# Another head for an attention + MLP kernel: loads by head, masks in fewer passes, weights behind values, and two engines in written order until the third pair

## The chip, the core and the metric

The kernel runs on one core of a Trainium2 chip. The metric is the device time of one execution in microseconds (us). The core has five engines that run side by side and meet at semaphores: TensorE (PE; its weight loads are shown apart as PEld), VectorE (DVE), ScalarE (ACT), GpSimd (POOL) and SyncE (SP), which here issues nearly all transfers. Lower is better.

## The reference

Attention of 4 batches x 8 heads x 768 positions x 64, with a mask and a bias by distance, followed by a two-layer MLP with a gate:

```python
scores = scale * np.matmul(q, k.transpose(0, 1, 3, 2))
keep = is_global | is_local            # first 8 keys, or the last 96 positions up to the query
scores = scores + bias                 # -slope[h] * distance
scores = np.where(keep, scores, -1000000000.0)
a = np.exp(scores - np.max(scores, axis=-1, keepdims=True))
attn = np.matmul(a / (np.sum(a, axis=-1, keepdims=True) + 1e-09), v)
x = attn.transpose(0, 2, 1, 3).reshape(B * S, H * D)      # 3072 x 512
h = x @ w_in                                              # 512 -> 2048
out = (h * np.clip(h + 3.0, 0.0, 6.0) / 6.0) @ w_out      # 2048 -> 512
```

The numbers `n_global` and `n_local` arrive as data, so the masks are built on the chip from a small transfer (`iv`).

## The kernel before, in words

The 3072 rows are 8 blocks of 384 rows (three tiles of 128). Attention of a block is done by pairs of heads, four pairs to a block, so pairs 0 to 11 are the first three blocks (`EARLY` = 12). For each tile t of a pair there are these steps:

- `scores(t)`: TensorE multiplies queries and keys of both heads (L765); VectorE adds the distances `p0` or `p1` of each head and takes the row's least value in one instruction (L776); ScalarE takes the exponential and the row's sum (L780).
- `sum_up` and `normalize`: VectorE adds 1e-9 and takes the reciprocal (L788, L789); the rows are multiplied by it, on VectorE for pair 0 (L796) and on GpSimd for all others (L798).
- `turn(t)`: TensorE transposes the rows (L806, L808), ScalarE copies them out (L810).
- `values`: TensorE multiplies with the values (L850), ScalarE and VectorE split the result into a high and a low part (L150, L151).

The first pairs run in a skewed loop `for n in range(-2, EARLY + 1)`: turn n holds `distances(n + 2)` (for n + 2 < 4), `scores` of pair n + 2, `sum_up` and `normalize` of pair n + 1, `turn` of pair n and `values` of pair n - 1. `distances` scales the masks `d0` and `d1` by each head's slope: three of pair 0's four on ScalarE (L323), all others on GpSimd (L325).

In the head before that loop, `rooms` zeroes half of the query columns of three load buffers on VectorE (L281), `iv` is fetched on ScalarE's queue, the first loads are issued on SP (three transfers for each pair: keys, queries of head 0, queries of head 1), and `banded_masks` makes `d0` and `d1` on VectorE (L263 to L274).

Meanwhile the MLP's weights are decoded: 32 chunks of 512 KB (`wst`, fetched on SP, two buffers), each by a magnitude on ScalarE (L362), six VectorE passes (L381, L394, L400, L409, L384, L398), a copy on ScalarE (L406) and a last VectorE pass (L391). Chunk 2f belongs to the first layer of slice f (`first`, L164), chunk 2f + 1 to the second (`second`, L196). A ledger (`work`) decides where in the written program a decode step stands: the first one stands at the values of turn n = 2. Chunk i + 2 can be fetched only after L384 of chunk i has read its buffer.

What sets the order: TensorE, SP and GpSimd keep the written order from the loop on (`in_order`). ScalarE and VectorE are ordered by the compiler's scheduler, which plays the program through on a timeline of its own and lets whatever is ready there go first. On the chip each engine then runs its list strictly in that order.

From turn n = 8 on, slices of the first block's MLP stand between the pairs; after the pairs, the MLPs of blocks 0 and 1 run, then blocks 2 to 7 with the next block's attention between their slices.

Of the kernel before, what the change touches and what calls it, by code (L numbers as in the profile page):

```python
# [33 lines left out]
QW = 2 * TB  # L34
VW = 2 * NT * P
LOAD = KW + QW + VW
NEG = 1.0e9
# [7 lines left out]
ROOMS = 2  # L45
MORE = 3
LEAD = 5.0
FIRST = 5

# [7 lines left out]
class Kernel:  # L57
# [189 lines left out]
    def banded_masks(self, pool):  # L247


        nc = self.nc  # L250
        c = self.const
        d0 = self.d0 = c.tile([P, P], F32, name="d0")
        d1 = self.d1 = c.tile([P, W], F32, name="d1")
        glo = c.tile([P, NG], F32, name="glo")
        rel, far = (pool.tile([P, W], F32, name=name) for name in ("rel", "local"))
        iota = dict(allow_small_or_imprecise_dtypes=True)
        nc.gpsimd.iota(far[:, CB:W], pattern=[[-1, P]], base=0, channel_multiplier=1, **iota)
        nc.gpsimd.affine_select(out=rel[:, CB:W], in_=far[:, CB:W], compare_op=ALU.is_ge, fill=FAR, base=0,
                                pattern=[[-1, P]], channel_multiplier=1)
# [3 lines left out]
        nc.vector.tensor_copy(out=fv, in_=self.iv)  # L263
        ng, nl = fv[:, 0:1], fv[:, 2:3]
        ts, tt = nc.vector.tensor_scalar, nc.vector.tensor_tensor
        ts(out=glo, in0=glo, scalar1=ng, scalar2=FAR, op0=ALU.is_ge, op1=ALU.mult)
        for d, cols in ((d0, slice(CB, W)), (d1, slice(0, W))):
            ts(out=far[:, cols], in0=rel[:, cols], scalar1=nl, scalar2=FAR, op0=ALU.is_ge, op1=ALU.mult)
            tt(out=d, in0=rel[:, cols], in1=far[:, cols], op=ALU.max)
            if d is d0:  # L270
                ts(out=glo, in0=glo, scalar1=nl, scalar2=None, op0=ALU.max)
                tt(out=d[:, 0:NG], in0=d[:, 0:NG], in1=glo, op=ALU.min)
            else:
                nc.vector.tensor_copy(out=d[:, PREV:CB], in_=glo)  # L274

    def rooms(self, pool, n, start=0):

        room = [pool.tile([P, LOAD], F32, name=f"load{start + i}") for i in range(n)]
        for i, at in enumerate(room):
            for j in range(2):  # L280
                self.nc.vector.memset(at[(1 - j) * D:(2 - j) * D, KW + j * TB:KW + (j + 1) * TB], 0.0)  # L281
        return room

# [3 lines left out]
    def load(self, n, values):  # L287


        if n < len(self.blocks) * NPAIR:  # L290
            parts = [(slice(KW + QW, LOAD), slice(None))] if values else [(slice(0, KW + QW), slice(None))]
            if n < EARLY and not values:
                parts = [(slice(0, KW), slice(None))] + [(slice(KW + j * TB, KW + (j + 1) * TB), slice(j * D, (j + 1) * D)) for j in range(2)]
            for columns, rows in parts:
                self.nc.sync.dma_start(out=self.place(n)[rows, columns], in_=self.pairs[n, rows, columns])

# [7 lines left out]
    def loaded(self, n):  # L304


        at = self.place(n)
        q = at[:, KW:KW + QW].rearrange("p (j t c) -> p j t c", j=2, t=NT)
        v = at[:, KW + QW:LOAD].rearrange("p (s t c) -> p s t c", s=2, t=NT)
        return at[:, 0:KW], q, v[:, 0], v[:, 1]  # L310

# [27 lines left out]
    def banded_setup(self):  # L339
# [3 lines left out]
        self.blocks = [(b, tb) for b in range(B) for tb in range(NTB)]  # L343
        self.room = self.rooms(self.const, ROOMS)
        self.iv = self.const.tile([P, 4], I32, name="iv")
        nc.scalar.dma_start(out=self.iv, in_=self.bounds.broadcast_to([P, 4]))
# [4 lines left out]
        with self.tc.tile_pool(name="scratch", bufs=1) as pool:  # L351
            self.banded_masks(pool)


# [103 lines left out]
    def banded(self, flag):  # L458

        self.banded_setup()  # L460
# [102 lines left out]
        self.finish()  # L563
        self.in_order(start)
        return acc

    def in_order(self, start):

        last = {}
        for i in self.nc.cur_bb.bb.instructions[start:]:  # L570
            if i.engine in (mybir.EngineType.PE, mybir.EngineType.SP, mybir.EngineType.Pool) and "Tile" not in type(i).__name__:
# [3 lines left out]
                last[i.engine] = i.name  # L575

# [136 lines left out]
class Pair:  # L713
# [14 lines left out]
    def split(self, step, load=True):  # L728
# [5 lines left out]
        for j, part in enumerate(self.parts):  # L734
# [3 lines left out]
            if step == 0:  # L738
                part["q1"] = kk.hp.tile([P, NT, P], F32R, name="q1")
                part["q2"] = kk.hp.tile([P, NT, P], F32R, name="q2")  # L740
                part["kx"] = kk.hp.tile([P, KW], F32R, name="kx")
                nc.scalar.mul(out=part["q1"], in_=q[:, j], mul=scale)
                nc.gpsimd.tensor_scalar(out=part["kx"][own, c], in0=k[own, c], scalar1=1.0, scalar2=0.0,  # L743
                                        op0=ALU.mult, op1=ALU.add)
            elif step == 1:
                nc.vector.scalar_tensor_tensor(out=part["q2"], in0=q[:, j], scalar=scale, in1=part["q1"].bitcast(F32),
                                               op0=ALU.mult, op1=ALU.subtract)
# [6 lines left out]
    def scores(self, t):  # L754
# [8 lines left out]
        for j in range(2):  # L763
            if self.plain:
                nc.tensor.matmul(sp[:, j, lo:W], lhsT=queries[:, j, t], rhs=keys[:, c], start=True, stop=True)  # L765
            else:
# [105 lines left out]
def pair_loads(q, k, v):  # L872

    pairs = np.zeros((B * NTB * NPAIR, P, LOAD), q.dtype)
    tile_rows = lambda p: np.concatenate([np.arange(p - PREV, p), np.arange(NG)]).clip(0)
    n = 0
    for b in range(B):  # L880
        for a in range(0, S, TB):
            cols = np.concatenate([np.arange(a - PREV, a).clip(0)]
                                  + [np.concatenate([np.arange(NG), np.arange(p, p + P)]) for p in range(a, a + TB, P)])
            for h in range(0, H, 2):
                qt, kt = (x[b, h:h + 2].transpose(0, 2, 1) for x in (q, k))
                at = pairs[n]
                at[:, 0:KW] = kt[:, :, cols].reshape(P, KW)
                for j in range(2):
                    for half in range(2):
                        if n >= EARLY or half == j:  # L890
                            at[half * D:(half + 1) * D, KW + j * TB:KW + (j + 1) * TB] = qt[j, :, a:a + TB]
                vt = v[b, h:h + 2].transpose(1, 0, 2).reshape(S, P)
# [35 lines left out]
```

## Time and profile before

| | |
|---|---|
| median of 3 runs | 675.11 us (674.5 to 675.69) |
| the profiled execution | 674.97 us, its span 673.1 us, clock 0.998 |
| TensorE busy | 655.3 us, 97% of the span |
| VectorE busy | 438.3 us, 65% |
| ScalarE busy | 283.0 us, 42% |
| GpSimd busy | 192.9 us, 29% |
| first matmul | 4.22 us after the span's start |

Times of the trace are counted from the span's start. TensorE's busy time is modelled from pipelined matmuls, so a busy TensorE is not always one at its peak; its idle time, 17.8 us, is the more telling number. A row of the timeline gives start, length, engine, line, operation, output and input, and in brackets how long the engine had been idle and who ended the wait; rows are merged where the same operation follows itself.

### The profile page before, as it was taken

How to read it: one execution, taken by the hardware profiler on the slowest of the kernel's cores; microseconds unless marked ns; L12 is line 12 of the kernel's file. 1: busy time of each engine (PE TensorE's matmuls, PEld its weight loads, DVE VectorE, ACT ScalarE, POOL GpSimd, SP SyncE). 2: the span in 40 equal slices, each digit the busy share in tenths (PEclk: the TensorE clock that was granted, in tenths of full speed). 3: DMA queues.
4: the chain of work that ended last, by engine and by line, in shares of the span. 5: the costliest groups of instructions: out<-in, count | busy, mean ns of one | idle time of the engine just before them, and what ended most of it. 6: DMA issues, size and time to landing. Idle time of an engine off the chain costs nothing.

```text
span 673.1 us, 11323 instructions
## 1 busy us (share of the span) xinstructions
PE 655.3 (97%) x3905; PEld 588.5 (87%) x3905; DVE 438.3 (65%) x1186; ACT 283.0 (42%) x744; POOL 192.9 (29%) x354
## 2 busy tenths in 40 slices
PE   5999999999999999999999999999999999999996
PEld 4788889999999889899989999899989999989995
DVE  7789999999975666457653676447762666422221
ACT  6998755544446333144333433143331443131111
POOL 2765500000000443234340343315431343302110
PEclk9999999999999999999999999999999999999999
DMA  8677533333303456624654367534555255510001
GB/s 259 164 226 242 162 121 102 118 108 112 95 31 133 131 135 181 157 94 131 167 139 119 101 172 193 144 94 126 139 159 140 80 151 141 139 48 1 1 1 52
DMA packets 62611, 84.33 MB, mean 125 GB/s; under 512 B 8784, under 2 KB 48720, under 8 KB 62544
## 3 DMA queue, kind: packets, MB, share of 16 engines
q1 hardware_dynamic: 62256, 83.25, 43.1%
q8 instruction: 33, 0.54, 0.3%
q14 instruction: 34, 0.28, 0.1%
q10 hardware_dynamic: 288, 0.26, 0.1%
HBM read 62.52 MB, written 20.97 MB: 124 GB/s over the span
## 4 chain that ended last, share of the span: by engine, by line
PE 87%; DMA 4%; ACT 4%; DVE 2%; POOL 2%; issue 1%; SPq 0%; POOLq 0%; ACTq 0%
PE hp L164 38%; PE acc L196 32%; DMA wst<-w 4%; PE xp L850 2%; PE sp L769 2%; PE tp L850 2%; PE sp L196 2%; PE tp L196 2%; PE xp L196 2%; PE tp L769 2%; ACT n L780 2%; POOL n L798 1%; PE acc L765 1%; ACT pt L810 1%; PE acc L850 1%
## 5 line engine op out<-in xcount | busy, mean ns | idle before, releaser
L175 ACT ACTIVATE g<-hp,small 128x384 f32<-128x384 f32 x127 | 73.9, 582 | 256.2 <-PE hp L164 221.2
L164 PE MATMUL hp<-xh,w1h 128*128 128x384 f32 x512 | 174.0, 340 | 0.0
L164 PE MATMUL hp<-xh,w1l 128*128 128x384 f32 x512 | 172.8, 337 | 0.0
L164 PE MATMUL hp<-xl,w1h 128*128 128x384 f32 x512 | 171.9, 336 | 0.0
L182 POOL TENSOR_SCALAR gh<-g 128x384 fp32r<-128x384 f32 x96 | 57.8, 602 | 294.8 <-DVE g L176 264.9
L196 PE MATMUL acc<-w2h,gl 128*128 128x512 f32 x336 | 132.9, 395 | 0.1
L196 PE MATMUL acc<-w2l,gh 128*128 128x512 f32 x336 | 132.8, 395 | 0.0
L196 PE MATMUL acc<-w2h,gh 128*128 128x512 f32 x336 | 132.1, 393 | 0.0
L798 POOL TENSOR_SCALAR n<-n,sums 128x232 f32<-128x232 f32 (+1 forms) x186 | 105.0, 581 | 52.3 <-DVE sums L789 38.7
L176 DVE SCALAR_TENSOR_TENSOR g<-g,hp 128x384 f32<-128x384 f32 x128 | 70.2, 548 | 76.4 <-ACT g L175 75.9
L780 ACT ACTIVATE n<-n,least 128x232 f32<-128x232 f32 (+1 forms) x192 | 89.5, 468 | 39.2 <-DVE least L776 38.5
L189 DVE TENSOR_TENSOR gl<-g,gh 128x384 fp32r<-128x384 f32 x128 | 73.1, 571 | 45.7 <-POOL gh L182 44.1
L164 PEld LDWEIGHTS hp<-xh,w1h 128*128 128x128 f32 x512 | 96.3, 188 | 5.5 <-issue 1.5
L164 PEld LDWEIGHTS hp<-xl,w1h 128*128 128x128 f32 x512 | 96.2, 188 | 3.8
L164 PEld LDWEIGHTS hp<-xh,w1l 128*128 128x128 f32 x512 | 96.0, 188 | 0.0
L196 PEld LDWEIGHTS acc<-w2l,gh 128*128 128x128 f32 x336 | 63.0, 188 | 13.3
L196 PEld LDWEIGHTS acc<-w2h,gl 128*128 128x128 f32 x336 | 63.2, 188 | 11.8 <-DVE gl L189 1.5
L196 PEld LDWEIGHTS acc<-w2h,gh 128*128 128x128 f32 x336 | 63.3, 188 | 10.6 <-POOL gh L182 0.3
L823 DVE STREAM_TRANSPOSE blocks<-n 128x256 f32<-128x256 f32 x112 | 43.5, 424 | 25.7 <-POOL n L798 25.1
L743 POOL TENSOR_SCALAR kx<-load 64x504 fp32r<-64x504 f32 (+1 forms) x40 | 23.1, 577 | 119.2 <-PE hp L164 117.6
L776 DVE CUSTOM_DVE_ANT_0 n<-sp,d 128x232 f32<-128x232 f32 (+1 forms) x70 | 23.7, 376 | 37.1 <-PE sp L769 36.8
L780 ACT ACTIVATION_READ_ACCUMULATOR n<-n,least 128x1 f32 x192 | 36.5, 190 | 0.0
(111 smaller groups left out, 764.9 us busy)
## 6 DMA issues: line engine op xcount, KB each, us to landing
wst<-w SPq DMA_DIRECT2D x32, 512.0 KB, 3.5
there<-blocks SPq DMA_DIRECT2D x52, 256.0 KB, 2.6
load<-pairs SPq DMA_DIRECT2D x20, 636.0 KB, 5.3
load<-pairs SPq DMA_DIRECT2D x32, 384.0 KB, 4.1
weights<-there SPq DMA_DIRECT2D x48, 192.0 KB, 3.8
out<-o SPq DMA_DIRECT2D x23, 256.0 KB, 2.1
weights<-there SPq DMA_DIRECT2D x32, 160.0 KB, 3.3
load<-pairs SPq DMA_DIRECT2D x12, 252.0 KB, 4.5
```

What stands on the lines that cost most here:

```text
L164: self.nc.tensor.matmul(hp, lhsT=self.w1(w, f)[:, kt, :], rhs=a[:, kt, :], start=(n == 0), stop=(n == 3 * NKT - 1))
L175: nc.scalar.activation(out=g, in_=hp, func=AF.Relu, bias=self.three, scale=1.0)
L176: nc.vector.scalar_tensor_tensor(out=g, in0=g, scalar=6.0, in1=hp, op0=ALU.min, op1=ALU.mult)
L182: self.nc.gpsimd.tensor_scalar(out=gh, in0=g, scalar1=1.0, scalar2=0.0, op0=ALU.mult, op1=ALU.add)
L189: self.nc.vector.tensor_tensor(out=gl, in0=g, in1=gh.bitcast(F32), op=ALU.subtract)
L196: self.nc.tensor.matmul(acc[tt], lhsT=a[:, tk], rhs=self.w2(w, f), start=(f == 0 and j == 0), stop=(f == NF - 1 and j == 2))
L769: nc.tensor.matmul(sp[:, j, lo:W], lhsT=q[:, t], rhs=part["kx"][:, c], start=(m == 0), stop=(m == 1))
L776: nc.vector.tensor_tensor_reduce(out=e[:, j, lo:W], in0=sp[:, j, lo:W], in1=d, op0=ALU.add, op1=ALU.min, scale=scale, scalar=3.0e38, accum ...
L780: nc.scalar.activation(out=e[:, j, lo:W], in_=e[:, j, lo:W], func=AF.Exp, bias=self.least[:, i:i + 1], scale=-1.0, accum_out=self.sums[:, ...
L798: nc.gpsimd.tensor_scalar(out=e[:, j, lo:W], in0=e[:, j, lo:W], scalar1=over, scalar2=0.0, op0=ALU.mult, op1=ALU.add)
L823: nc.vector.transpose(out=blocks[:, :, s].rearrange("p b j q -> p j b q"), in_=e[:, :, c:c + P].rearrange("p j (b q) -> p j b q", b=4))
L850: nc.tensor.matmul(xps[j * D:(j + 1) * D, t * P:(t + 1) * P], lhsT=vt[0:K, t, j * D:(j + 1) * D], rhs=self.part(t, j, c, K), start=(c == 0 ...
```

## The change

- The load buffer is laid out anew: queries of head 1, keys, queries of head 0. So each head's keys and queries are one contiguous run of columns in that head's 64 partitions, and a pair's load is two transfers instead of three, each to 64 partitions. For pair 0 the second goes on ScalarE's queue.
- The zeroing moves: two memsets of buffer 0 stay on VectorE, those of buffers 1 and 2 go to GpSimd.
- The masks: the comparison with `n_local` is one VectorE pass over 232 columns instead of two (128 and 232); the two small passes over `glo` and a copy go to GpSimd.
- `wake` issues four small matmuls on a constant before any data is there.
- SP's order: loads of pair 2, values of pair 0, weights chunk 0, values of pair 1, weights chunk 1 (before: chunk 0, loads of pair 2, chunk 1, values of pairs 0 and 1).
- ScalarE and VectorE keep the written order from the very start until turn n = 1 begins (`HEAD` = 1), which is up to the scores of pair 2, the sums of pair 1 and the transposes of pair 0; everything later on these two engines comes behind that.

```diff
+KQ = TB + KW
+HEAD = 1
+WAKE = 4
@@ banded_masks
-        ts(out=glo, in0=glo, scalar1=ng, scalar2=FAR, op0=ALU.is_ge, op1=ALU.mult)
-        for d, cols in ((d0, slice(CB, W)), (d1, slice(0, W))):
-            ts(out=far[:, cols], in0=rel[:, cols], scalar1=nl, scalar2=FAR, op0=ALU.is_ge, op1=ALU.mult)
-            tt(out=d, in0=rel[:, cols], in1=far[:, cols], op=ALU.max)
-            if d is d0:
-                ts(out=glo, in0=glo, scalar1=nl, scalar2=None, op0=ALU.max)
-                tt(out=d[:, 0:NG], in0=d[:, 0:NG], in1=glo, op=ALU.min)
-            else:
-                nc.vector.tensor_copy(out=d[:, PREV:CB], in_=glo)
+        pool_ts = nc.gpsimd.tensor_scalar
+        pool_ts(out=glo, in0=glo, scalar1=ng, scalar2=FAR, op0=ALU.is_ge, op1=ALU.mult)
+        pool_ts(out=glo, in0=glo, scalar1=nl, scalar2=0.0, op0=ALU.max, op1=ALU.add)
+        ts(out=far, in0=rel, scalar1=nl, scalar2=FAR, op0=ALU.is_ge, op1=ALU.mult)
+        tt(out=d0, in0=rel[:, CB:W], in1=far[:, CB:W], op=ALU.max)
+        tt(out=d0[:, 0:NG], in0=d0[:, 0:NG], in1=glo, op=ALU.min)
+        tt(out=d1[:, 0:PREV], in0=rel[:, 0:PREV], in1=far[:, 0:PREV], op=ALU.max)
+        tt(out=d1[:, CB:W], in0=rel[:, CB:W], in1=far[:, CB:W], op=ALU.max)
+        nc.gpsimd.tensor_copy(out=d1[:, PREV:CB], in_=glo)
@@ rooms
-        for i, at in enumerate(room):
-            for j in range(2):
-                self.nc.vector.memset(at[(1 - j) * D:(2 - j) * D, KW + j * TB:KW + (j + 1) * TB], 0.0)
+    def blank(self, room, engine):
+        engine.memset(room[D:P, KQ:KW + QW], 0.0)
+        engine.memset(room[0:D, 0:TB], 0.0)
@@ load
-                parts = [(slice(0, KW), slice(None))] + [(slice(KW + j * TB, KW + (j + 1) * TB), slice(j * D, (j + 1) * D)) for j in range(2)]
+                parts = [(slice(TB, KW + QW), slice(0, D)), (slice(0, KQ), slice(D, P))]
             for columns, rows in parts:
-                self.nc.sync.dma_start(out=self.place(n)[rows, columns], in_=self.pairs[n, rows, columns])
+                engine = self.nc.scalar if n == 0 and rows == slice(D, P) else self.nc.sync
+                engine.dma_start(out=self.place(n)[rows, columns], in_=self.pairs[n, rows, columns])
@@ banded_setup
         self.room = self.rooms(self.const, ROOMS)
+        self.blank(self.room[0], nc.vector)
...
             self.banded_masks(pool)
+        self.blank(self.room[1], nc.gpsimd)
+    def wake(self):
+        any_ = self.three.broadcast_to([P, P])
+        out = self.ps_x.tile([P, BANK], F32, name="xp")[:, 0:P]
+        for _ in range(WAKE):
+            self.nc.tensor.matmul(out, lhsT=any_, rhs=any_, start=True, stop=True)
@@ banded
+        begin = here()
         self.banded_setup()
-        start = len(self.nc.cur_bb.bb.instructions)
+        start = here()
...
+        self.wake()
...
-            self.fetch(0)
...
+                self.blank(self.room[2], self.nc.gpsimd)
                 self.load(2, False)
+                self.load(0, True)
+                self.fetch(0)
+                self.load(1, True)
                 self.fetch(1)
-                for n in range(ROOMS):
-                    self.load(n, True)
...
                 for n in range(-2, EARLY + 1):
+                    if n == HEAD:
+                        head = here()
...
-        self.in_order(start)
+        self.in_order(start, here(), (mybir.EngineType.PE, mybir.EngineType.SP, mybir.EngineType.Pool))
+        self.in_order(begin, head, (mybir.EngineType.Activation, mybir.EngineType.DVE), True)
```

More of the change, by code (lines that the diff above doesn't have):

```diff
@@ L265, in banded_masks @@
         ts, tt = nc.vector.tensor_scalar, nc.vector.tensor_tensor
[L266 to L282 removed]
+        pool_ts = nc.gpsimd.tensor_scalar
[7 more added lines that the diff above has]
+        nc.gpsimd.tensor_copy(out=d1[:, PREV:CB], in_=glo)
+    def rooms(self, pool, n, start=0):
+        return [pool.tile([P, LOAD], F32, name=f"load{start + i}") for i in range(n)]
+    def blank(self, room, engine):
+        engine.memset(room[D:P, KQ:KW + QW], 0.0)
+        engine.memset(room[0:D, 0:TB], 0.0)
     def place(self, n):
@@ L307, in loaded @@
         at = self.place(n)
-        q = at[:, KW:KW + QW].rearrange("p (j t c) -> p j t c", j=2, t=NT)
+        q = [at[:, c].rearrange("p (t c) -> p t c", t=NT) for c in (slice(KQ, KW + QW), slice(0, TB))]
         v = at[:, KW + QW:LOAD].rearrange("p (s t c) -> p s t c", s=2, t=NT)
-        return at[:, 0:KW], q, v[:, 0], v[:, 1]
+        return at[:, TB:KQ], q, v[:, 0], v[:, 1]
     def plain_distances(self, ctx):
@@ L458, in banded @@
     def banded(self, flag):
+        here = lambda: len(self.nc.cur_bb.bb.instructions)
+        begin = here()
         self.banded_setup()
-        start = len(self.nc.cur_bb.bb.instructions)
+        start = here()
         self.common(2, 2)
@@ L563, in banded, with in_order @@
         self.finish()
-        self.in_order(start)
+        self.in_order(start, here(), (mybir.EngineType.PE, mybir.EngineType.SP, mybir.EngineType.Pool))
+        self.in_order(begin, head, (mybir.EngineType.Activation, mybir.EngineType.DVE), True)
         return acc
-    def in_order(self, start):
+    def in_order(self, start, end, engines, first=False):
         last = {}
-        for i in self.nc.cur_bb.bb.instructions[start:]:
-            if i.engine in (mybir.EngineType.PE, mybir.EngineType.SP, mybir.EngineType.Pool) and "Tile" not in type(i).__name__:
+        for n, i in enumerate(self.nc.cur_bb.bb.instructions[start:None if first else end], start):
+            if i.engine in engines and "Tile" not in type(i).__name__:
                 if i.engine in last:
@@ L574, in in_order @@
                         mybir.DependencyClass.NoSync, mybir.DependencyReason.DATA), reason="in_order")
-                last[i.engine] = i.name
+                if n < end:
+                    last[i.engine] = i.name
     def attention(self, i, x, first):
@@ L741, in split @@
                 part["kx"] = kk.hp.tile([P, KW], F32R, name="kx")
-                nc.scalar.mul(out=part["q1"], in_=q[:, j], mul=scale)
+                nc.scalar.mul(out=part["q1"], in_=q[j], mul=scale)
                 nc.gpsimd.tensor_scalar(out=part["kx"][own, c], in0=k[own, c], scalar1=1.0, scalar2=0.0,
@@ L745, in split @@
             elif step == 1:
-                nc.vector.scalar_tensor_tensor(out=part["q2"], in0=q[:, j], scalar=scale, in1=part["q1"].bitcast(F32),
+                nc.vector.scalar_tensor_tensor(out=part["q2"], in0=q[j], scalar=scale, in1=part["q1"].bitcast(F32),
                                                op0=ALU.mult, op1=ALU.subtract)
@@ L764, in scores @@
             if self.plain:
-                nc.tensor.matmul(sp[:, j, lo:W], lhsT=queries[:, j, t], rhs=keys[:, c], start=True, stop=True)
+                nc.tensor.matmul(sp[:, j, lo:W], lhsT=queries[j][:, t], rhs=keys[:, c], start=True, stop=True)
             else:
@@ L886, in pair_loads @@
                 at = pairs[n]
-                at[:, 0:KW] = kt[:, :, cols].reshape(P, KW)
+                at[:, TB:KQ] = kt[:, :, cols].reshape(P, KW)
                 for j in range(2):
@@ L890, in pair_loads @@
                         if n >= EARLY or half == j:
-                            at[half * D:(half + 1) * D, KW + j * TB:KW + (j + 1) * TB] = qt[j, :, a:a + TB]
+                            at[half * D:(half + 1) * D, slice(KQ, KW + QW) if j == 0 else slice(0, TB)] = qt[j, :, a:a + TB]
                 vt = v[b, h:h + 2].transpose(1, 0, 2).reshape(S, P)
```

## The prediction, made before the changed kernel was run

> **What bounds the kernel now.** I read the page first, then the windows, then the timeline of the first 25 us.
>
> ```profile
> span 673.1 us, 11323 instructions
> PE 655.3 (97%) x3905; PEld 588.5 (87%) x3905; DVE 438.3 (65%) x1186; ACT 283.0 (42%) x744; POOL 192.9 (29%) x354
> ```
>
> TensorE is idle for 673.1 - 655.3 = 17.8 us; that, and matmuls that run slowly, is all there is to win. The windows (busy time of PE, PEld, DVE, ACT, POOL, then clock, transfer share, GB/s) say where it lies:
>
> ```profile
> 0.00:5.00 5.00, 0.78 (x3) 0.60 (x3) 3.28 (x13) 1.49 (x2) 1.41 (x10) 1.00 0.51 152
> 10.00:15.00 5.00, 2.57 (x16) 1.82 (x15) 4.05 (x23) 4.79 (x18) 0.00 (x0) 1.00 1.03 344
> 15.00:20.00 5.00, 3.87 (x23) 2.74 (x22) 5.00 (x22) 4.64 (x19) 2.88 (x4) 1.00 0.85 237
> 30.00:35.00 5.00, 5.00 (x45) 4.44 (x45) 3.05 (x16) 4.20 (x16) 3.65 (x9) 1.00 0.87 261
> 45.00:50.00 5.00, 4.88 (x43) 3.93 (x44) 3.64 (x16) 5.00 (x18) 3.91 (x8) 1.00 0.79 253
> ```
>
> In the three early stretches TensorE idles 4.22 + 2.43 + 1.13 = 7.8 us; later it is full, and ScalarE beside it (4.20, then 5.00 of 5). So the head is bound by what feeds TensorE. The timeline shows which work that is:
>
> ```profile
> 0.73 0.41 ACTq L346 DMA_DIRECT2D iv<-bounds  x1
> 0.73 3.44 SPq L295 DMA_DIRECT2D load<-pairs  x6
> 1.00 2.89 DVE L281 MEMSET load<- 64x384 f32 x6
> 3.89 0.17 DVE L263 CAST fv<-iv 128x4 f32<-128x4 int32 x1
> ...
> 5.16 0.51 ACT L323 ACTIVATE p<-d 128x128 f32<-128x128 f32 x2 [2.49 <-DVE d L272]
> 5.84 0.29 DVE L776 CUSTOM_DVE_ANT_0 n<-sp,p 128x128 f32<-128x128 f32 x1
> 6.53 2.84 POOL L325 TENSOR_SCALAR p<-d 128x232 f32<-128x232 f32 x9 [4.55 <-DVE d L274]
> 6.96 0.38 ACT L323 ACTIVATE p<-d 128x232 f32<-128x232 f32 x1
> 7.41 0.40 DVE L776 CUSTOM_DVE_ANT_0 n<-acc,p 128x232 f32<-128x232 f32 x1
> ...
> 10.21 0.67 ACT L362 ACTIVATE wz<-wst 128x512 f32<-128x512 f32 x1 [1.78 <-DMA wst<-w]
> 10.91 0.43 DVE L381 TENSOR_SCALAR wz<-wz 128x512 f32<-128x512 f32 x1 [1.12 <-ACT wz L362]
> 11.50 0.40 DVE L776 CUSTOM_DVE_ANT_0 n<-acc,p 128x232 f32<-128x232 f32 x1
> 11.82 0.40 DVE L776 CUSTOM_DVE_ANT_0 n<-acc,p 128x232 f32<-128x232 f32 x1
> 12.14 0.42 DVE L394 TENSOR_SCALAR wz<-wz 128x512 int32<-128x512 int32 x1
> 13.67 0.69 DVE L400 SCALAR_TENSOR_TENSOR wz<-wst,wz 128x512 int32<-128x512 int32 x1
> 13.91 0.64 ACT L362 ACTIVATE wz<-wst 128x512 f32<-128x512 f32 x1
> 14.27 0.59 DVE L796 TENSOR_SCALAR n<-n,sums 128x232 f32<-128x232 f32 x2
> 15.61 0.42 DVE L381 TENSOR_SCALAR wz<-wz 128x512 f32<-128x512 f32 x1
> 15.95 0.42 DVE L409 TENSOR_SCALAR we<-wz 128x512 int32<-128x512 int32 x1
> 16.91 0.16 DVE L789 RECIPROCAL sums<-sums 128x2 f32<-128x2 f32 x1
> 17.12 4.30 POOL L798 TENSOR_SCALAR n<-n,sums 128x128 f32<-128x128 f32 x6 [7.75 <-DVE sums L789]
> 21.50 1.94 POOL L325 TENSOR_SCALAR p<-d 128x128 f32<-128x128 f32 x4
> 21.84 0.29 DVE L776 CUSTOM_DVE_ANT_0 n<-sp,p 128x128 f32<-128x128 f32 x1 [1.18 <-POOL p L325]
> 24.41 0.68 PE L806 MATMUL tp<-ident,n 128*128 128x128 f32 x2 [0.15 <-POOL n L798]
> ```
>
> The reader is to see two things. ScalarE stands 1.78 us before weights that nothing needs yet (10.21), with pair 0's remaining exponentials queued behind it, and VectorE stands 1.12 us behind that. And GpSimd idles 7.75 us until VectorE gives pair 1's sums; then its own chain runs without a break: normalizing pair 1 (17.12), the distances of pair 3 (21.50), normalizing pair 2, for which TensorE's transposes wait at 24.41. What brings 17.12 forward brings 24.41 forward.
>
> **The change, part by part, counted to GpSimd's start at 17.12.** The first answer on transfers comes ahead (size, us from issue to landing), with two rows of TensorE:
>
> ```profile
> load<-pairs SPq DMA_DIRECT2D x1, 252.0 KB, 3.0
> iv<-bounds ACTq DMA_DIRECT2D x1, 2.0 KB, 3.1
> ...
> load<-pairs SPq DMA_DIRECT2D x1, 252.0 KB, 7.4
> ```
> ```profile
> 5.48 3.06 PE L765 MATMUL acc<-load 128*128 128x232 f32 x8
> 8.82 1.73 PE L765 MATMUL acc<-load 128*128 128x232 f32 x8
> ```
>
> *Memsets and masks.* `iv`, issued at 0.73, lands at 3.83; the six memsets end at 3.89, so taking four off VectorE wins only 0.06. `d0` needs one pass of 232 columns where it had passes of 128 and 8; I put L323 at 5.1 instead of 5.16. The rest of `d1` has one pass less on VectorE, so the first L776 starts near 5.5 instead of 5.84. More matters that ScalarE's scaling of `d1` for head 0 no longer stands behind exponentials (6.96 to 7.34): in written order it runs from about 5.65, and the second tile's L776 starts near 6.15 instead of 7.41: **1.26 us**. The small passes over `glo` lie on an idle GpSimd (4.55 us before 6.53). So do its four memsets: between 4 x 0.38 = 1.5 us (VectorE's 64x384, 2.89 for six with their gaps) and 4 x 0.52 = 2.1 us (a pass of L325, 2.84 / 9 = 0.32, by 384 / 232 columns). I take nothing, since they depend on nothing and can run in that gap; the other end, 2.1 us, is for the case that they stand behind the masks.
>
> *Written order.* No decode step is written before turn n = 2, so all of it leaves the head. VectorE loses the wait of 1.12 and five passes, which cost 0.4 to 0.6 each: **2.1 us**. And pair 1's first sums come ahead of one tile of pair 2's L776 (0.64, two at the pitch 11.50 to 11.82). Together 1.26 + 1.12 + 2.1 + 0.64 = 5.1 us. The same forward from 6.15: pair 0's two tiles, four L776 at 0.32, 1.28; turn n = -1 with six L776 (1.7), three sums (1.0, an estimate from L789's 0.16 twice) and three normalizations (3 x 0.59); then pair 2's first tile and pair 1's sums, 0.75. That ends at 12.65, 4.5 us before 17.12; the 0.6 between the two is what the mixed order overlapped. I take 4.5. ScalarE keeps up: its exponentials of pairs 0 to 2 and three copies end near 16.3.
>
> *Transfers and TensorE's start.* Pair 0's second part goes out on ScalarE's queue behind `iv` near 1.15 and lands near 4.2; the third transfer of before went out near 1.9 (3.44 / 6 each) and landed near 4.9. That wins little, for early matmuls are slow: eight passes take 3.06 us, later 1.73. Slow, the third tile's scores end near 8.3, where VectorE wants the last of them near 7.3 (6.15, three pitches of 0.32 and a semaphore's delay): 1.0 us lost. If `wake` (eight passes of 128 columns, 3.06 x 128 / 232 = 1.7 us, from 1.0 on) has TensorE fast by 4.5, nothing is lost. I take half, 0.5: GpSimd starts near 13.1, **4.0 us** earlier (ends 3.5 and 5.1; 1.9 with the memsets misplaced).
>
> [...]
>
> *Weights behind values.* Chunk 0 was there at 10.21; pair 2's load (252 KB of keys and 2 x 64 x 384 x 4 bytes, 444 KB) and pair 0's values (128 x 768 x 4 bytes) now go ahead, 2.4 us at the 344 GB/s shown. Its cover is that decoding starts behind VectorE's head, near 15. Cost: none.
>
> *What is late next.* The moved decoding must go where the engines are fuller: two magnitudes on ScalarE (0.67 + 0.64 = 1.31 us), some 5 us of passes on VectorE. VectorE has 1.95 us free in 30 to 35, 1.36 in 45 to 50, and a gap from about 15.1 until pair 3's distances at 17.6. ScalarE has 0.80 in 30 to 35 and about 1.3 in that gap. This nearly covers both; I charge 0.4. Sum: 4.0 - 0.4 = **3.6 us**. The profiled execution took 674.97 us (its span and 1.9 around it), 0.14 below the median of 675.11; 675.11 - 3.6 = **671.5 us**.
>
> The shift outlives the pairs only if weights are decoded in time:
>
> ```profile
> 27.54 0.69 DVE L391 TENSOR_TENSOR w2l<-we,w2h 128x512 fp32r<-128x512 f32 x1
> ...
> 35.03 0.68 ACT L362 ACTIVATE wz<-wst 128x512 f32<-128x512 f32 x1 [0.83 <-DMA wst<-w]
> ...
> 84.27 0.68 DVE L391 TENSOR_TENSOR w1l<-we,w1h 128x512 fp32r<-128x512 f32 x1
> ...
> 87.12 0.42 PE L164 MATMUL hp<-xh,w1h 128*128 128x384 f32 x1
> ```
>
> Chunk 8 is ready at 84.95 and used at 87.12, the narrowest margin, 2.2 us. But the chain of chunks moves with the head too, since fetches stand in SP's order among loads that wait for TensorE, and it has a hole from chunk 1's end at 28.2 to chunk 2's start at 35.0.
>
> **The rivals.** *Loads by halves land late.* If 64 partitions take data at half the rate, a pair's 444 KB take 2.6 us instead of 1.3 at 344 GB/s, and pair 3's load (now issued after 8.3, landing 7.4 later, near 15.7; then about 1 us sooner) comes four times 1.3 us later, near 20, where its rows are wanted near 17.5: 2.5 us lost, 674.0. For it: the transfers are saturated there (share 1.03). Against: the halves follow each other and may overlap. [...]
>
> *ScalarE swallows it.* It is full at 45 to 50; if the moved 1.31 us and one more stall before weights, like the 1.78, land there, 3.1 of the 4.0 go: 674.2, no measurable change.
>
> *The decode chain decides (slower).* If chunk 1 ends at 38.5 instead of 28.2, the hole is used up, chunk 8 comes 3.5 us late, its use slips 1.3 us past 87.12 and every block with it: 676.5, and 1 us more for each further us. It takes 10 us of delay, while what moved is some 5 us of passes; unlikely.
>
> **How the numbers follow.** This kernel's runs can tell 0.2%, 1.35 us, from no change. Forecast (2.6 to 5.4 us won) 0.54; half-rate loads or ScalarE taking part of it (1.35 to 2.6 won) 0.20; the same two taking nearly all 0.15; the decode chain 0.11. So faster 0.74, same 0.15, slower 0.11. The low end, 669.7, is the full 5.1 and a little of TensorE's later idling; the high end, 674.8, takes in both swallowing rivals and the misplaced memsets.
>
> **What would show it.** Right: no L362 before 15; GpSimd's first L798 near 13; transposes of pair 2 near 20.4; the L164 of 87.12 some 3.6 us sooner, and likewise all that follows. `wake` right: L765's eight at about 1.8 us instead of 3.06. Wrong: TensorE waiting on `load`, GpSimd's memsets between masks and L325, or L164 waiting for L391 near 83.

## The result, and the profile after

The changed kernel takes **684.88 us** (683.59 to 685.03), where the kernel before, run beside it, took 675.4: a ratio of 1.0133, interval 1.0116 to 1.015. It is 9.5 us slower; 3.6 us faster was forecast. A fourth execution, at a mean granted clock of 0.657, took 922.34 us; it counts in this median (684.74 without it), not in the range or the ratio. The profiled execution took 683.59 us. Page of the changed kernel:

```profile
span 681.6 us, 11332 instructions
PE 659.4 (97%) x3913; PEld 592.7 (87%) x3913; DVE 435.1 (64%) x1179; ACT 283.1 (42%) x744; POOL 192.3 (28%) x361
```

The first three windows of 5 us as before, and 25 to 30 (busy time of PE, PEld, DVE, ACT, POOL, then clock, transfer share, GB/s):

```profile
0.00:5.00 5.00, 2.07 (x8) 1.78 (x8) 1.73 (x7) 1.49 (x2) 3.95 (x17) 1.00 0.55 125
10.00:15.00 5.00, 5.00 (x29) 4.79 (x28) 4.47 (x27) 3.72 (x17) 0.00 (x0) 1.00 1.04 352
15.00:20.00 5.00, 4.55 (x38) 3.44 (x38) 3.44 (x24) 4.62 (x19) 2.99 (x8) 1.00 0.98 250
25.00:30.00 5.00, 2.52 (x18) 1.91 (x14) 5.00 (x18) 4.70 (x19) 0.54 (x1) 1.00 0.73 193
```

From 10 to 20 TensorE is far fuller than before (9.55 against 6.44 us). Then it pays back: 2.52 in 25 to 30, where VectorE has no free time. These rows lie there:

```profile
28.48 0.68 DVE L398 SCALAR_TENSOR_TENSOR we<-wst,we 128x512 f32<-128x512 uint32 x1
29.09 0.18 DVE L812 RECIPROCAL sums<-sums 128x6 f32<-128x6 f32 x1
...
30.13 0.68 PE L829 MATMUL tp<-ident,n 128*128 128x128 f32 x2 [2.60 <-POOL n L821]
```

The transposes of pair 3 wait for GpSimd, GpSimd for pair 3's sums (L812), and VectorE comes to these only behind passes of chunks 0 and 1, which it does side by side from 21.41 on. No transfer is late here. Pair 2's transposes had come 1.9 us sooner than before (22.47, 24.41 before); pair 3's come 0.5 later (30.13, 29.60 before). So the head's win is gone by then. Windows of 20 us, first of the kernel before, then of the changed one, show where the balance turns:

```profile
0.00:20.00 20.00, 12.22 (x58) 9.79 (x58) 16.38 (x80) 13.17 (x47) 7.13 (x23) 1.00 0.82 248
20.00:40.00 20.00, 19.45 (x166) 16.82 (x167) 16.26 (x71) 17.88 (x61) 13.36 (x28) 1.00 0.67 192
40.00:60.00 20.00, 18.65 (x160) 16.14 (x159) 18.38 (x70) 19.70 (x66) 12.32 (x22) 1.00 0.80 235
60.00:80.00 20.00, 19.51 (x155) 17.09 (x154) 18.85 (x56) 14.81 (x42) 10.48 (x16) 1.00 0.53 167
80.00:100.00 20.00, 19.30 (x128) 16.88 (x127) 19.19 (x39) 11.78 (x22) 2.41 (x3) 1.00 0.45 145
```
```profile
0.00:20.00 20.00, 15.86 (x84) 13.88 (x86) 11.33 (x67) 12.45 (x46) 9.93 (x34) 1.00 0.90 248
20.00:40.00 20.00, 17.38 (x146) 14.96 (x143) 19.68 (x75) 18.77 (x62) 12.72 (x22) 1.00 0.66 178
40.00:60.00 20.00, 18.22 (x160) 15.74 (x159) 15.60 (x67) 15.90 (x52) 12.01 (x24) 1.00 0.75 216
60.00:80.00 20.00, 15.61 (x110) 13.68 (x109) 16.17 (x50) 15.61 (x46) 6.34 (x12) 0.91 0.53 174
80.00:100.00 20.00, 18.28 (x142) 16.01 (x140) 17.12 (x37) 11.59 (x25) 4.66 (x6) 1.00 0.44 127
```

In the first 20 us TensorE idled 7.78 us before and, if the 2.07 of `wake` (which does no work) counts as idle, 6.21 now: the head won 1.6. From 20 to 100 it idled 3.09 before and 10.51 now: 7.4 lost, over half of it (3.9) from 60 to 80, where the granted clock also fell to 0.91. ScalarE's gate of block 1, slice 0 comes at 106.75 instead of 99.30; the remaining 1.0 of the 8.5 us that the span grew lies behind it and was not followed.

Rows of the changed kernel's timeline for the head:

```profile
0.91 2.07 PE L366 MATMUL xp<-small 128*128 128x128 f32 x8 [0.91 <-DVE small L104]
...
3.44 0.42 POOL L286 MEMSET load<- 64x384 f32 x1
...
5.76 1.19 PE L788 MATMUL sp<-load 128*128 128x128 f32 x4 [2.78 <-DMA load<-pairs]
...
7.11 0.29 DVE L799 CUSTOM_DVE_ANT_0 n<-sp,p 128x128 f32<-128x128 f32 x1 [1.65 <-PE sp L788]
...
16.36 0.73 POOL L821 TENSOR_SCALAR n<-n,sums 128x128 f32<-128x128 f32 x2 [7.90 <-ACT n L803]
...
19.88 1.26 ACT L376 ACTIVATE wz<-wst 128x512 f32<-128x512 f32 x2
```

GpSimd's memsets fitted its gap, and no magnitude stands before 15. But the first scores wait for their load until 5.76 (4.22 before), and GpSimd starts at 16.36: 0.76 earlier than before, not 4.0. The transfers are one reason (the written order, below, is another): two windows (the last two columns are the transfers' busy share and GB/s), then size and us from issue to landing in the first 30 us:

```profile
4.50:9.75 5.25, 3.98 (x12) 3.67 (x13) 1.77 (x11) 2.37 (x10) 3.38 (x11) 1.00 1.02 254
9.75:13.50 3.75, 3.75 (x20) 3.56 (x20) 3.04 (x19) 2.96 (x13) 0.00 (x0) 1.00 1.04 407
```
```profile
load<-pairs SPq DMA_DIRECT2D x15, 222.0 KB, 5.0
...
load<-pairs ACTq DMA_DIRECT2D x1, 222.0 KB, 4.5
```

From 4.5 to 9.75 us, where most of what has been issued are halves (six of ten transfers, `iv` aside), 254 GB/s move at full share (1.02); when values and weights, which go to all partitions, follow, 407 at the same share (1.04). The two rates point to slower halves. They don't show it alone, nor that the rate is half: the kernel before, whose queries also go to 64 partitions, moves 261 GB/s from 4.5 to 9.75 at a share of 0.90.

Later on, these are three further waits of TensorE:

```profile
60.14 0.66 ACT L376 ACTIVATE wz<-wst 128x512 f32<-128x512 f32 x1 [2.63 <-DMA wst<-w]
...
63.06 0.30 PE L829 MATMUL tp<-ident,n 128*128 128x128 f32 x1 [1.69 <-ACT pt L833]
...
71.47 0.64 DVE L398 SCALAR_TENSOR_TENSOR we<-wst,we 128x512 f32<-128x512 uint32 x1
73.72 0.66 ACT L376 ACTIVATE wz<-wst 128x512 f32<-128x512 f32 x1 [2.44 <-DMA wst<-w]
74.42 0.43 DVE L395 TENSOR_SCALAR wz<-wz 128x512 f32<-128x512 f32 x1 [2.30 <-ACT wz L376]
75.83 0.39 DVE L799 CUSTOM_DVE_ANT_0 n<-sp,p 128x232 f32<-128x232 f32 x1
76.60 1.92 PE L788 MATMUL sp<-load 128*128 128x232 f32 x4 [2.70 <-DVE least L799]
...
92.51 0.66 ACT L376 ACTIVATE wz<-wst 128x512 f32<-128x512 f32 x1 [2.62 <-DMA wst<-w]
...
94.19 0.30 PE L829 MATMUL tp<-ident,n 128*128 128x128 f32 x1 [1.72 <-ACT pt L833]
```

Read it from 71.47 on. ScalarE has nothing in front of it but a magnitude whose weights land at 73.72; VectorE's next instruction is that chunk's first pass; behind it stand two passes that were ready or waited for ScalarE, and then L799, the distances of a pair, whose scores have been there since 72.2. TensorE cannot reuse the score bank until L799 has read it, so it stands 2.70 us. The four matmuls that follow take 1.92 us instead of 1.05. So a late transfer stopped three engines (2.44, 2.30 and 2.70 us) by way of what stands behind its first users. (In the kernel before, too, the three exponentials from 10.78 on, for which VectorE was done by 9.37, ran behind the magnitude of 10.21.)

Who waits behind these magnitudes in the first 110 us, before and then now (us, times):

```profile
ACT wz L362: 10.1, 11
DVE wz L381: 2.7, 5
```
```profile
ACT wz L376: 13.6, 8
DVE wz L395: 9.1, 6
```

ScalarE stood before weights in the kernel before, too. What grew most is VectorE's share: 2.7 to 9.1 us.

### The profile page after: what moved, and what is told of

Its sections match the earlier page's. It is cut to its first block, busy times and chain, and to the rows that moved or that the text cites. A ratio compares the mean times of both kernels' runs of the same rounds, so it can differ in the third digit from the quotient of the medians.

```text
span 681.6 us, 11332 instructions
## 1 busy us (share of the span) xinstructions
PE 659.4 (97%) x3913; PEld 592.7 (87%) x3913; DVE 435.1 (64%) x1179; ACT 283.1 (42%) x744; POOL 192.3 (28%) x361
## 4 chain that ended last, share of the span: by engine, by line
PE 85%; DVE 5%; DMA 5%; ACT 2%; issue 1%; POOL 1%; POOLq 0%; ACTq 0%; SPq 0%; DVEq 0%
PE hp L167 37%; PE acc L199 32%; DMA wst<-w 4%; PE xp L873 3%; PE sp L792 2%; PE tp L873 2%; PE tp L792 2%; PE sp L199 1%; PE tp L199 1%; PE xp L199 1%; PE acc L788 1%; DVE n L799 1%; POOL n L821 1%; PE sp L788 1%; DMA load<-pairs 1%
## 5 line engine op out<-in xcount | busy, mean ns | idle before, releaser
L821 POOL TENSOR_SCALAR n<-n,sums 128x232 f32<-128x232 f32 (+1 forms) x186 | 102.5, 568 | 60.6 <-DVE sums L812 47.1
L799 DVE CUSTOM_DVE_ANT_0 n<-sp,d 128x232 f32<-128x232 f32 (+1 forms) x70 | 23.7, 376 | 36.8 <-PE sp L792 36.5
```

The lines of the kernel that those rows point to most:

```text
L799: nc.vector.tensor_tensor_reduce(out=e[:, j, lo:W], in0=sp[:, j, lo:W], in1=d, op0=ALU.add, op1=ALU.min, scale=scale, scalar=3.0e38, accum ...
L821: nc.gpsimd.tensor_scalar(out=e[:, j, lo:W], in0=e[:, j, lo:W], scalar1=over, scalar2=0.0, op0=ALU.mult, op1=ALU.add)
```

## The experiments

Each ratio is to the kernel before, run beside it on the same chip; microseconds of gain or loss are differences to that kernel's median. The theories: (1) the sequence of ScalarE's and VectorE's instructions costs the time, (2) the transfers by halves do, by landing late (2a) or by making the scheduler choose another sequence (2b). Two more came up on the way: (3) the round trip of the two raw buffers carries the loss, (4) ready work stands behind a pass whose weights are late.

### Parts alone

| run | edit | median us | ratio (95%) |
|---|---|---|---|
| e1_no_order | the change without ScalarE's and VectorE's written order | 681.23 | 1.0084 (1.006 to 1.0107) |
| e2_order_only | before, with that order alone | 677.12 | 1.003 (1.0013 to 1.0047) |
| e3_loads_whole | the change with the old three loads | 678.7 | 1.0057 (1.0032 to 1.0081) |
| e4_weights_first | the change with weights fetched in the old place | 683.2 | 1.0109 (1.0064 to 1.0154) |
| e5_loads_only | before, with loads by head alone | 681.73 | 1.0088 (1.0063 to 1.0113) |
| e6_rest_only | the change without order and with old loads: masks, memsets, `wake`, weights behind values | 678.15 | 1.0031 (1.0014 to 1.0049) |

```diff
# e1, e6
-        self.in_order(begin, head, (mybir.EngineType.Activation, mybir.EngineType.DVE), True)
# e3, e6; e5 is the reverse, in the kernel before
-                parts = [(slice(TB, KW + QW), slice(0, D)), (slice(0, KQ), slice(D, P))]
+                parts = [(slice(0, KW), slice(None))] + [(slice(KW + j * TB, KW + (j + 1) * TB), slice(j * D, (j + 1) * D)) for j in range(2)]
# e4
-                self.load(2, False)
-                self.load(0, True)
                 self.fetch(0)
-                self.load(1, True)
+                self.load(2, False)
                 self.fetch(1)
+                for n in range(ROOMS):
+                    self.load(n, True)
```

> The changed kernel without the written order of ScalarE and VectorE; all its other edits stay. Theory 1 (order): holding all decoding out of the head bunches two chunks' passes on VectorE right behind it, where TensorE needs VectorE for the pairs, and the loss of some 9 us is that; then this kernel takes 673 to 676 us. Theory 2 (transfers): the loss is from loads by head landing later (first scores at 5.8 instead of 4.2) and from the weights behind the values; then it stays at 681 to 685.

> The kernel before with the written order of ScalarE and VectorE until turn 1 as its only edit. Theory 1: slower than before by 5 to 10 us (680 to 685), with VectorE full from 20 to 40 and TensorE waiting there for normalized rows. Theory 2: the head gains 3 to 4 us as predicted and it takes 671 to 674.

> The changed kernel with each pair's load as before (keys over 128 partitions, then the two queries, all on SP). Theory 1: the first scores start about 1.5 us earlier, near 4.2, and little of it remains at the end: 682 to 685. Theory 2: most of the loss goes, 674 to 678.

> The changed kernel with weights chunks 0 and 1 fetched as early as before. Theory 1: decoding still cannot start before the head's end near 19, when both chunks were there in any case: 683 to 686, no change. Theory 2: chunk 0 is there some 2 us sooner and the stalls before weights shrink: 677 to 681.

> The kernel before with loads by head as its only edit (the new layout, two transfers of 64 partitions a pair, pair 0's second on ScalarE's queue; six memsets on VectorE as before). So far loads by head cost about 6 us in the company of the other edits. Theory 2 (transfers): they do it alone, 679 to 682, with the first scores near 5.7. Rival: they cost only together with the other edits, 674 to 677.

> The changed kernel without the written order and with whole loads: what is left are masks in fewer passes, memsets on GpSimd, the early matmuls and the weights behind the values. If the parts add up, 674 to 677. Rival: weights behind values (or another of these) carries a loss of its own, 678 or more.

Every part alone costs: loads by head 5.8 us, the order 1.7, the rest 2.2. That this adds up to 9.7, next to the 9.5, is in part luck: loads and rest together (e1) cost 5.8 and not 8.0, order and rest together (e3) 3.3 and not 3.9. Of the expectations, e2 missed both of its ranges and e3 that of theory 2 by 0.7 us. e6's row on GpSimd is the most telling: its first normalization starts at 13.19, as forecast for the whole change, and the kernel is slower all the same. e3 is e6 with the written order: there GpSimd starts at 15.18. e4's interval overlaps that of the change, so the place of the weights is not decided by it.

### Written order through all pairs

e8_order_pairs is e2 with `HEAD = EARLY`, e9_order_pairs_loads that with loads by head.

> The kernel before with ScalarE and VectorE in written order until turn 12, through all pairs, as its only edit. Theory 1a: the loss comes from the seam, where the scheduler bunches the decoding that was held back; without a seam the ledger spreads it, and the head's win stays: 670 to 674. Theory 1b: VectorE is simply too full for the pairs with decoding behind the head, wherever it stands: 677 to 681.

> As the run with written order through all pairs, and loads by head beside it. Every engine's list of compute is then the same in both, so the difference is that of the transfers alone. Theory 2a: transfers to 64 partitions move slower, weights land later behind them: 3 to 6 us over the run without them. Theory 2b: the loads cost through another order that the scheduler chose for them: within 1.5 us of it.

Measured: 701.51 us (1.0379, 1.0344 to 1.0413) and 702.41 (1.0387, 1.0364 to 1.041). e8 missed both of its ranges. Holding two engines to the written order everywhere costs 26 us; ScalarE waits 26.4 us for VectorE's distances (L784 in that kernel) in the first 130. So decoding spread by the written program is far worse than decoding bunched behind the third pair. That the bunching is free does not follow: with the order alone (e2), TensorE has the wait of 30.13 too,

```profile
28.91 0.68 PE L814 MATMUL tp<-ident,n 128*128 128x128 f32 x2 [2.08 <-POOL n L806]
```

and without it (e1) no wait over 0.95 us from 20 to 40. Loads by head cost only 0.9 here, but a kernel with so much idle time can hide a late transfer.

### The same sequence, other transfers

Here ScalarE's and VectorE's instructions are chained into a given sequence, by rank in the written program:

```diff
+    def impose(self):
+        ...
+        for engine, order in ORDERS.items():
+            own = written[engine]
+            for a, b in zip(order, order[1:]):
+                self.tc.add_manual_dep(own[b], own[a].name, ..., reason="impose")
```

> The kernel before with the loads by head, as in the run with that one part (681.73, +5.8 us), but ScalarE and VectorE are held to the very sequence of instructions that they have in the kernel before; only the transfers differ, and both halves of pair 0 are issued from the sync queue. If the loads cost time because they land later and slower (2a), this stays at 680 to 683. If they cost time because the scheduler, which places instructions by its own guess of the transfers, then writes ScalarE and VectorE in another order (2b), this comes back to 675 to 677.5, the first scores still late at about 5.8 us.

> The mirror of it: the kernel before with its own whole loads, but ScalarE and VectorE held to the sequence that the scheduler chose for the loads by head. By 2a (transfers) this is the kernel before again, 674.5 to 677. By 2b (the chosen sequence) it loses what the loads lost: 679.5 to 682.5, with the loads landing as early as before.

> The changed kernel with everything that it has (loads by head, masks in fewer passes, GpSimd's memsets, wake, weights behind the values), but in place of its written order ScalarE and VectorE are held to the sequence of the kernel before; the three mask passes that are new stand where their inputs put them. If the whole loss of 9.5 us is a matter of which instruction stands before which (2b for the loads, the same for the rest), this is 673 to 677, and the first normalization on GpSimd still comes well before 17. If the transfers cost (2a), 680 to 683.

> The changed kernel without its written order and with whole loads, as in the run of the rest alone (678.15, +2.2 us), but ScalarE and VectorE are held to the sequence of the kernel before. By 2b this takes the prediction's gain without the loss: 671.5 to 674.5, the first normalization near 13. If masks, wake and weights behind the values cost by themselves (late first weights, a TensorE that is slow all the same), it stays at 677 to 679.

| run | loads | sequence | median us | ratio (95%) |
|---|---|---|---|---|
| (e5 above) | by head | its own | 681.73 | 1.0088 |
| e11_loads_old_schedule | by head | of before | 677.08 | 1.0022 (1.001 to 1.0034) |
| e12_whole_new_schedule | whole | of e5 | 678.62 | 1.0041 (1.0028 to 1.0053) |
| e13_after_old_schedule | the change | of before | 678.61 | 1.0053 (1.0033 to 1.0074) |
| e14_rest_old_schedule | rest, whole | of before | 679.36 | 1.006 (1.0042 to 1.0078) |

Contrary to what was expected of e11, the second half of pair 0 went out on ScalarE's queue there as in e5, so the two differ in the sequence alone. Neither theory alone holds. With the transfers changed and the sequence kept, loads by head cost 1.7 us; with the sequence changed and the transfers kept, 3.3; with both, 5.8. (e12 and e13 lie between their two ranges. No run holds the kernel before to its own sequence, so that the chaining itself costs nothing was not tested.) In e12, with whole loads, two waits of TensorE stand where e5 has them, at 19.29 and 77.97:

```profile
19.52 0.48 PE L822 MATMUL hp<-ident,n 128*128 128x128 f32 x1 [3.81 <-DVE n L812]
...
75.88 1.63 PE L781 MATMUL sp<-load 128*128 128x232 f32 x4 [1.77 <-DVE least L792]
```

The first is not that of a late transfer: VectorE and ScalarE are busy without a gap from 15.5 to 19.5, and the new sequence brings pair 0's last normalization up late.

e13 returns 6.2 of the 9.5 us by sequence alone, though its GpSimd starts at 18.44, later than in the kernel before. e14 missed: it was to gain and lost 4.0. The old sequence has chunk 0's magnitude eighth on ScalarE, and with weights behind values the chunk is not there:

```profile
13.03 0.66 ACT L377 ACTIVATE wz<-wst 128x512 f32<-128x512 f32 x1 [4.30 <-DMA wst<-w]
```

It is again a magnitude that stands before its transfer, with the exponentials of the first pairs behind it.

### Three raw buffers, and the masks alone

```diff
-            self.decoding(words, 2, 2, side="right")
+            self.decoding(words, 3, 2, side="right")
-                if i + 1 < N:
-                    self.fetch(i + 1)
+                if i + 2 < N:
+                    self.fetch(i + 2)
+            elif a:
+                self.fetch(2)
```

> The changed kernel, whole, with three buffers for raw weights instead of two: the fetch of chunk 2 is issued with chunk 0's first pass, and each later fetch two chunks ahead instead of one. If the loss, wherever it begins, is carried to the end of the head by the round trip of a raw buffer (VectorE has read it, the sync queue comes to the fetch, 6 us of landing, magnitude, six passes; theory 3), the waits of ScalarE for weights (12.1 us in the first 110 us) nearly go and this gives back more than half of the loss: 675 to 680. If the sequence of VectorE alone holds the chain (theory 1), or the shared transfers (theory 2, which then has one more transfer in the crowded stretch), it stays at 682 to 687.

> The same third raw buffer in the kernel before, where ScalarE waits 10.1 us for weights in the first 110 us. By theory 3 it gains there too, 670 to 674, and less than in the changed kernel, where landings are longer. By theories 1 and 2 no change, 674 to 677.

> The kernel before with the masks in fewer passes and the memsets of rooms 1 and 2 on GpSimd, and nothing else of the change: loads whole, weights fetched in the old place, no wake, no written order. The rest of the change as a whole cost 2.2 us (678.15) though GpSimd began 4 us sooner, and its first weights came 3.3 us later (13.49 instead of 10.21). If the later weights cost that, this is the gain of the prediction without it: 671 to 674. If an earlier start of GpSimd is worth nothing because the chain of weights sets the end, 674.5 to 676.5. If the scheduler's sequence for it is worse by chance, 677 to 680.

e15: 686.68 us (1.0172, 1.0155 to 1.0188). e16: 679.81 (1.0062, 1.0048 to 1.0076), above both of its ranges. Fetching earlier made both kernels slower, so the round trip of a buffer does not carry the loss: theory 3 fell. Earlier fetches run beside the loads and land later (median 6.1 us in e15, 4.8 in the changed kernel), and the wait is where it was:

```profile
77.90 1.91 PE L790 MATMUL sp<-load 128*128 128x232 f32 x4 [2.44 <-DVE least L801]
```

e17 (the masks and the memsets on GpSimd): 676.66 us (1.0014, 1.0005 to 1.0023), between two of its ranges and no change that counts. GpSimd starts 1.76 us earlier, and further on the same chain of waits eats it:

```profile
15.36 0.82 POOL L818 TENSOR_SCALAR n<-n,sums 128x128 f32<-128x128 f32 x2 [6.86 <-DVE sums L809]
...
70.39 0.67 ACT L375 ACTIVATE wz<-wst 128x512 f32<-128x512 f32 x1 [2.26 <-DMA wst<-w]
...
72.26 1.05 PE L785 MATMUL sp<-load 128*128 128x232 f32 x4 [1.63 <-DVE least L796]
```

### Moving only the passes that stand

The sequence of the changed kernel (e18) and of e17 (e19), with these moves and nothing else:

```diff
# e18, ScalarE, chunks 3, 5, 7 (chunk 10: behind gh and pt)
-  wz(c), xh or gh, pt, w1h, ...
+  xh or gh, pt, w1h, wz(c), ...
# e18, VectorE, chunk 7 (3, 5 and 10 likewise)
-  L395(c), L412, L192, L799, L799, L408(c), ...
+  L412, L192, L799, L799, L395(c), L408(c), ...
# e19, chunk 7 alone: four places back on both engines
```

> The changed kernel, whole, ScalarE and VectorE held to the very sequence that they have in it, but for four chunks of weights (3, 5, 7 and 10, whose magnitudes stood on ScalarE 1.61, 2.63, 2.44 and 2.62 us for a transfer): their magnitude goes two or three places back on ScalarE, behind the casts and copies that were queued behind it, and their first pass two to four places back on VectorE, behind the passes that were ready. Transfers, TensorE, GpSimd and the sync queue are untouched. Theory 4: the loss is the work of the attention standing behind a pass whose weights are late; it returns TensorE's idle 1.69 (63.06), 2.70 (76.60) and 1.72 (94.19) and the slow matmuls after 76.60 (about 1.6): 7.7 at most, 677 to 681 with what comes late next. If the chain of the weights itself sets the end (TensorE waits for weights instead), it stays at 683 to 687.

> The masks alone (676.66 us), with the same thing done to the one chunk whose magnitude stood 2.26 us there (chunk 7, at 70.39; TensorE then stood 1.63 before the scores at 72.26): four places back on ScalarE and on VectorE. By theory 4 this gives 1 to 1.6 us back and is the first version under the kernel before: 674.5 to 675.7. If TensorE is held by something else as soon as this wait is gone, 676 to 677.5.

e18: 678.97 us, 1.0059 (1.0045 to 1.0073), against 1.0133 (1.0116 to 1.015) for the change: nine moved instructions (in chunk 5, L408 goes along) return 5.8 of the 9.5 us. Theory 4 holds for the larger part. The same moves were not tried on the kernel before, so part of the 5.8 may be a gain that any sequence would give; e19 below, the nearest to it, gains 0.2 us, within its noise. The wait of 30.13 stays (2.59, at 29.82). Of the three waits at 63, 76 and 94, the last row of these is left:

```profile
45.30 0.68 ACT L378 ACTIVATE wz<-wst 128x512 f32<-128x512 f32 x1 [3.44 <-DMA wst<-w]
...
50.31 0.33 PE L843 MATMUL tp<-ident,n 128*128 128x128 f32 x1 [3.41 <-POOL n L835]
...
76.72 1.05 PE L802 MATMUL sp<-load 128*128 128x232 f32 x4 [0.42 <-DVE least L813]
```

The first two rows show the same thing by accident: in this profiled execution chunk 3, issued at 36.81, took 8.5 us to land, its first pass stood all the same, and the execution took 683.00 us where the four others of this kernel took 678.24 to 680.54. What cost it that is open: the others have no trace, and its granted clock was also 0.66 in 30 to 35 and in 50 to 55. e19: 675.97 us, 1.0008 (0.9997 to 1.0019), against e17's 1.0014 (1.0005 to 1.0023): TensorE's wait of 1.63 is gone from the trace; the excess over the kernel before fell from 0.9 to 0.7 us, but the intervals overlap. It ties with the kernel before; no version run here beats that.

### A hole of TensorE, filled

```diff
+                        if n == 0 and t == NT - 1:
+                            self.fill(11)      # 11 matmuls ident x ident into a bank that nothing reads
                         if 0 <= n < EARLY:
                             pairs[n].turn(t)
```

> Loads by head alone (681.73 us), ScalarE and VectorE held to the sequence of that run, with 11 idle matmuls of 128x128 (22 passes, about 2.7 us, results never read) put on TensorE into its hole from 15.47 to 19.29, ahead of pair 0's last transposes. After that hole the granted clock was 0.76 from 20 to 30 and a transpose took 0.42 instead of 0.27 until 26.5. If the hole made TensorE slow and that was on the path, the clock stays at 1.00, the transposes at 0.27, and 2 to 3.5 us come back: 678 to 680. If TensorE is slow for another reason, or its 3 us are waited for elsewhere, 681 to 683.

TensorE around the hole in loads by head alone (e5), with the window behind it, and then with the hole filled (e20):

```profile
19.29 0.48 PE L808 MATMUL hp<-ident,n 128*128 128x128 f32 x1 [3.82 <-DVE n L798]
19.56 0.42 PE L810 MATMUL hp<-ident,n 128*128 128x128 f32 x1
```
```profile
20.00:30.00 10.00, 10.00 (x72) 8.81 (x73) 8.10 (x32) 7.56 (x25) 7.90 (x15) 0.76 0.30 80
```
```profile
15.03 2.62 PE L363 MATMUL xp<-ident 128*128 128x128 f32 x22
19.01 0.33 PE L832 MATMUL hp<-ident,n 128*128 128x128 f32 x1 [1.36 <-DVE n L822]
19.18 0.27 PE L834 MATMUL hp<-ident,n 128*128 128x128 f32 x1
```
```profile
20.00:30.00 10.00, 9.51 (x84) 8.10 (x83) 8.18 (x34) 8.13 (x28) 8.63 (x18) 1.00 0.39 100
```

The clock stays at 1.00, the transposes at 0.27, and 84 matmuls instead of 72 fit into 20 to 30. The time is 679.43 us, 1.0067 (1.0053 to 1.0081), against e5's 1.0088 (1.0063 to 1.0113): 1.7 us by the medians, though the intervals overlap. That the hole slows TensorE is shown; the size of what it costs in the end is not.

## Why the prediction was wrong

**The count to GpSimd's start: the step that failed first.** It came to 4.0 us and measured 0.76. "What brings 17.12 forward brings 24.41 forward" held in the trace (22.47), and carried no further: pair 3's transposes already come later than before. Nor does the start set the time: e6 starts GpSimd at 13.19 and e17 at 15.36, and neither is faster. The prediction took the head's gain as the kernel's, less what is late next.

**What is late next: the term that was mis-sized.** It charged 0.4 us, by comparing busy time that moved with free time later, and let decoding start near 15. Measured, TensorE idles 7.4 us more from 20 to 100 and runs slowly for a part of 60 to 80. Decoding starts at 19.88 on ScalarE and at 21.41 on VectorE, for two chunks at once, and VectorE is full from 25 to 30: a wait of 2.60. Further on free time is not the limit (VectorE is busy 15.60 of 20 from 40 to 60): what counts is which pass stands in front of which when a chunk lands late. Four magnitudes stood 1.61 to 2.63 us each, where the kernel before has one so long past its head (1.83, at 62.38), and moving the four with their first passes on VectorE returned 5.8 us (e18). The row at 10.21, where ScalarE stood 1.78 before weights, was quoted and read as a cost to remove from the head; that the same can stand between any two passes, once the sequence is drawn anew, was not drawn from it.

**Transfers and TensorE's start.** Pair 0's second part was to land near 4.2; the first scores waited until 5.76, and with them the 1.26 us of the second tile were gone (L799 at 8.65, where 7.41 stood before). The rival of half-rate loads named what the rates point to (254 GB/s in the stretch of mostly halves, 407 behind it); half the rate for 64 partitions was the author's assumption, and no run shows it. It was priced for one load, pair 3's. That one came early enough (its L799 at 19.77 instead of 21.84); pair 0's paid, and fetches of weights land later beside the halves (in the first 110 us a median of 4.8 us, 4.3 before).

**Written order.** No magnitude before 15: right. It was the largest part of the count (1.12 + 2.1 + 0.64), yet e3 with it starts GpSimd 2.0 us later than e6 without it. Alone it costs 1.7 us (e2), with GpSimd at 15.24.

**`wake`.** It was half counted and does nothing: the next eight passes take 3.30 us, and 3.30 in e5, which has no `wake` (3.06 before). That matmuls ahead of the data make the first scores fast, for which half of 1.0 us was booked, was the author's estimate; no run shows it.

**Memsets** were right, at no cost. (VectorE stood 0.60 us for GpSimd's pass over `glo` at 4.92; the late scores hid it.) **Weights behind values, cost none**: undecided in the changed kernel (e4), wrong where a sequence wants them early (e14).

**The rivals.** *ScalarE swallows it* came nearest: it foresaw one more stall before weights. There were four, and VectorE and TensorE stood with ScalarE; its price, 674.2, was far too low. *The decode chain decides* had the right sign by luck, for a reason that did not occur: chunk 1's last pass began at 33.95, ahead of its 38.5, and loosening that chain (e15) made things worse.

**Open**: where the 1.7 us of e11 and the 3.3 of e13 lie, which keep the old sequence. Both have fetches that land later than in the kernel before (medians of 4.5 and 4.8 us), and VectorE stands longer behind magnitudes (4.3 and 6.8 us); moving single passes in them was not tried. What the wait of 30.13 is worth in the end was not tested either.

## What to carry to other kernels

Where ready work stands behind a pass that waits, as L799 did here until 75.83 with its scores there since 72.2, price an edit by asking for each instruction that waits for a transfer what stands right behind it, and who waits for that; shares of busy time do not show it. An edit that only moves a landing, or only makes a scheduler draw its order anew, can change these pairings everywhere behind it (alone, the two cost 1.7 us in e11 and 3.3 in e12), so a gain in the head must be followed to the end of the stage before it is booked. Work that is held back must go somewhere: bunched, it made one wait, of 2.60 us, that took the head's whole win. A pass whose data may be late belongs behind the work that is ready: nine instructions moved so were worth 5.8 us here, more than the 3.6 forecast for the whole change.

## What the runs showed of the hardware

- At full share, a stretch of mostly halves moved 254 GB/s (the change, 4.5 to 9.75 us), one of transfers to 128 partitions 407 (9.75 to 13.5).
- A hole of 3.82 us made TensorE's transposes follow at 0.42 instead of 0.27 us for some 6 us, at a granted clock of 0.76 in 20 to 30 (e5); with the hole filled they took 0.27, at 1.00 (e20). The four matmuls that take 1.05 us took 1.92 after a hole of 2.70 (the change; clock 0.66 in 75 to 80), 1.63 after 1.77 (e12), and 1.05 after 1.63 (e17). The length of a hole alone does not decide the clock in these runs: after the hole of 2.60 at 30.13 (the change) the granted clock is 1.00 in 30 to 35, after one of 2.59 at 29.82 (e18) it is 0.66.
- A fetch of 512 KB took 3.3 to 8.5 us from issue to landing within the first 110 us of a single execution (e18).
